# Attention ahead of a routed expert layer on one core: packed inputs, quarter-array scores, softmax sums from a column of ones, and a later weight split

## The chip, the cores and the metric

The kernel runs on one core of a Trainium2 chip. The metric is the device time in microseconds (us) of one execution. A core has five engines that run their own instruction streams side by side: PE (TensorE, matrix products into the accumulator banks called PSUM; PEld is its weight loading), DVE (VectorE), ACT (ScalarE), POOL (GpSimd) and SP (SyncE, which here issues the transfers). Sixteen DMA engines move the data that these streams ask for.

## What is computed

Three parts follow each other. First attention with 4 batches, 8 heads, 576 positions and 64 features a head, in a causal window of 64 positions. Then every one of the 2304 tokens goes to the one of 8 experts that its gate chooses (512 to 1024 to 512 features). Last comes a layer of 512 to 2048 to 512 features with the activation h * cos(h).

```python
def _attn_ref(q, k, v) -> np.ndarray:
    B, H, S, D = q.shape
    window = 64
    scale = 1.0 / np.sqrt(D)
    scores = scale * np.matmul(q, k.transpose(0, 1, 3, 2))
    pos = np.arange(S)
    rel = pos[:, None] - pos[None, :]
    mask = (rel >= 0) & (rel < window)
    scores = np.where(mask, scores, -1000000000.0)
    scores = scores - np.max(scores, axis=-1, keepdims=True)
    attn = np.exp(scores)
    attn = attn / (np.sum(attn, axis=-1, keepdims=True) + 1e-09)
    return np.matmul(attn, v).astype(np.float32)

def reference(**kwargs):
    ...
    x = np.ascontiguousarray(attn_out.transpose(0, 2, 1, 3)).reshape(B * S, H * D)
    x = _moe_ref(x=x, **moe_kwargs)
    return _moe2_ref(x=x, **moe2_kwargs)
```

## The kernel before

The attention works on 18 tiles of 128 tokens. A tile holds two blocks of 64 tokens (`c` is 0 or 1), and a block sees its own 64 keys and the 64 before it. The 8 heads are 4 pairs (`pr`), and `r` says which head of a pair. A loop over `t` runs a software pipeline: the scores of tile `t`, the transposes and the product with the values of tile `t - 1`, the gate's logits of tile `t - 2`, the routing of tile `t - 3`, and the id tables of tile `t - 4`. The order of the instructions on PE, DVE, ACT and SP is that of the program text (`manual_schedule`), so each of these engines works its list in order and waits at the first instruction that isn't ready.

What a tile does, with the lines of the kernel before:

- `load` (L150 to L152) fetches q of the one head of each pair, the keys (each tile its own and the 64 before, so keys between two tiles come twice), and q of the other head. `load_v` (L160) fetches the values in two transfers, one a block. The zeros of `qz` around a head's q let a product over all 128 rows give that head's scores alone. Loads run three tiles ahead, values two.
- `stA` (L173) makes 16 products of 128 rows and 64 columns, 128 wide. Each shows as two instructions, so 32 a tile. `peak` (L191, DVE) adds the mask and takes the maximum, `soft` (L207, ACT) is the exponential, and its accumulator gives the sum of a row in a second instruction (ACTIVATION_READ_ACCUMULATOR).
- `stB` (L223) transposes on PE, `evB` takes the first half out of PSUM on DVE (L230) and the second on ACT (L232), `stC` (L241) multiplies by the values, `norm` (L254 to L259, DVE) divides by the sums.
- `stD` and `stE` (L272 to L283) turn the tile and make the gate's logits; `route`, `gate`, `stF`, `rank` and `stH` find experts and ranks. GpSimd does two small operations a tile (L358, L360).
- Expert 0's weights come as four pieces `wst[c]` of 1 MB at tiles 1, 5, 9 and 13 (L515). Each piece is cut into quarters; of each quarter ACT makes the upper part (L577) and DVE, through `early_lo`, the rest (L115). The 16 quarters are spread over tiles 3 to 17.
- Products of a first slot of expert 0 (`work0`, L477) fill PE's gaps near the end. The last tile's ids go through `ids_part` (L387) and a product to the list `gix`; gathers by that list bring the first slot's tokens, and `mX` (L718) turns them. From there the expert part and the last part are PE work.

PSUM has 8 banks that all stages share in turn.

Of the kernel before, what the change touches and what calls it, by code (L numbers as in the profile page):

```python
# [17 lines left out]
P = 128  # L18
# [13 lines left out]
FILL = ((0, 4, 0, 0), (3, 3, 0, 2), (0, 4, 0, 4), (0, 0, 24, 0), (0, 0, 0, 0))  # L32
NS = NT - 1
# [4 lines left out]
ROW = DM + 1  # L38
NQ = N // P * E // 2
# [9 lines left out]
def kernel(ctx: ExitStack, tc: tile.TileContext, a: dict, out: bass.AP, dbg=None):  # L49
# [33 lines left out]

# [19 lines left out]
    # an expert's weights, as they come and as two parts of 12 bits; expert 0 ahead of the routing  # L103
# [10 lines left out]
    def split_lo(c, w=slice(0, 2048)):  # L114
        nc.vector.tensor_tensor(hl[c][:, 1, w], wst[c][:, w], hl[c][:, 0, w].bitcast(F32), op=ALU.subtract)  # L115

# [6 lines left out]
    # keeps the tensor engine's clock up while it has nothing else to do  # L123
# [8 lines left out]
    # a head's q, with zeros where the other head of its pair has its rows  # L132
    qz = [t4.tile([P, 2, 4, P], F32, name=f"qz{i}", bufs=1) for i in range(4)]
    for i in range(4):
        for r in range(2):
            nc.gpsimd.memset(qz[i][(1 - r) * D : (1 - r) * D + D, r], 0.0)

    def blkinfo(i):
        offs = []
        for c in range(2):  # L140
            b, jb = divmod(2 * i + c, 9)
            offs.append(b * SP + jb * D)
        return offs

    def load(i):
        o0, o1 = blkinfo(i)
        w = o1 - o0 + P
# [7 lines left out]
        st[i] = dict(q=q, k=k, off=(0, o1 - o0))  # L155

    def load_v(i):
        st[i]["v"] = v = t4.tile([P, 2, DM], F32, tag="v", name=f"v{i}", bufs=5)
        for c, o in enumerate(blkinfo(i)):
            nc.sync.dma_start(out=v[:, c, :], in_=a["v"][o : o + P, :])  # L160

    def stA(i):
# [8 lines left out]
        for r in range(2):  # L171
            for pr, c in ((pr, c) for pr in range(4) for c in range(2)):
                nc.tensor.matmul(  # L173
                    sb[r][c * D : c * D + D, pr * P : pr * P + P],
                    s["q"][:, r, pr, c * D : c * D + D],
                    s["k"][:, pr, s["off"][c] : s["off"][c] + P],
                    start=True,
                    stop=True,
                )
# [3 lines left out]
        s["su"] = sm.tile([P, 8], F32, tag="su", name=f"su{i}")  # L183
# [19 lines left out]
    def soft(i, r):  # L203
        s = st[i]
        for pr in range(4):
# [7 lines left out]
                accum_out=s["su"][:, hh : hh + 1],  # L213
# [12 lines left out]
    def evB(i, r):  # L226
        s = st[i]
        dst = s["pT"][:, r * 4 : r * 4 + 4, :].rearrange("p a b -> p (a b)")
        if r == 0:
            nc.vector.tensor_copy(dst, s["pb"][r])  # L230
        else:
            nc.scalar.activation(dst, s["pb"][r], AF.Copy)  # L232

    def stC(i):
        s = st[i]
        ob = psum(f"o{i}")
        for r in range(2):
            for pr in range(4):
                h = 2 * pr + r
# [8 lines left out]
        s["ob"] = ob  # L248

    def norm(i):  # L250
        s = st[i]
        ob = s["ob"]
        ri = sm.tile([P, 8], F32, tag="ri", name=f"ri{i}")
        nc.vector.tensor_scalar(ri, s["su"], 1e-9, None, ALU.add)  # L254
        yield
        nc.vector.reciprocal(ri, ri)
        yield
        xo = t2.tile([P, ROW], F32, tag="xo", name=f"xo{i}", bufs=5)
        nc.vector.tensor_tensor(  # L259
            xo[:, :DM].rearrange("p (a r d) -> p a r d", r=2, d=D),  # L260
            ob[:, :].rearrange("p (a r d) -> p a r d", r=2, d=D),
            ri[:, :].rearrange("p (r a) -> p a r", r=2).unsqueeze(3).to_broadcast([P, 4, 2, D]),
            op=ALU.mult,
        )
        s["xo"] = xo
        yield
# [10 lines left out]
    def stE(i):  # L277
# [6 lines left out]
        s["l"] = lb[:, :E]  # L284

    # steps of VectorE's, a step of another chain between each two of them
# [34 lines left out]
    # ids by expert and rank: a token's row of 128 ranks and its place there as 0 and 1,  # L321
    # summed over the tokens by a product, with the middle of the ids taken off
    idt = {}

    def stF(i):
        s = st[i]
        rb = psum(f"r{i}")
        nc.tensor.matmul(rb[:, :E], onesb, accs, start=True, stop=False)
# [754 lines left out]
```

## Time and profile before

| what | us |
|---|---|
| three runs, without a profile: median | 843.57 |
| lowest, highest | 839.75, 844.72 |
| span of the profiled execution, first to last instruction | 837.9 |

The page gives no time for the profiled execution other than its span; the three runs lie 1.9 to 6.8 us above it. The profile shows one execution: which instruction ran when on which engine, what an engine waited for, and what the DMA engines moved. A duration of one PE instruction includes the pipeline, so the pace is read from the starts. DMA share is the mean busy share of the 16 DMA engines; it can come out somewhat above 1.

### The profile page before, as it was taken

To read this page: it belongs to the slowest core of one execution; us is meant where nothing else is said; L and a number is where in the kernel's file an instruction comes from. 1 tells how busy PE (TensorE), PEld (TensorE's weight loads), DVE (VectorE), ACT (ScalarE), POOL (GpSimd) and SP (SyncE) were. 2 spreads that over 40 slices of the span, in tenths; PEclk is the share of its full clock that TensorE was granted. 3 is DMA by queue.
4 is the path that set the end of the run, shared out by engine and by line. 5 is a ranking of instruction groups with operands and counts; after the bars stand their busy time and mean duration, and the time that the engine had idled before them with its cause. 6 is when DMAs were issued, how large, how long until landed. Compare 5 with 4: busy or idle time off the path is not lost. (4 is left out here: it accounts for less than half of the span.)

```text
span 837.9 us, 15164 instructions
## 1 busy us (share of the span) xinstructions
PE 807.4 (96%) x5233; PEld 700.6 (84%) x5233; DVE 521.0 (62%) x1350; ACT 432.7 (52%) x1045; POOL 108.2 (13%) x119
## 2 busy tenths in 40 slices
PE   7897998999999999999899999999999999999995
PEld 5887876888888888888789999999999999999994
DVE  4786976688457479964378755555555555555552
ACT  5796863454344345453367654454545445445442
POOL 2221322122112122221000010010001001001001
PEclk9998999999999999999999999999999999999998
DMA  9999926889747689871335110100001010001001
GB/s 247 298 302 309 292 82 233 284 302 336 247 144 284 230 270 301 295 277 36 104 106 159 39 38 1 38 30 8 15 24 39 1 38 38 2 1 39 1 0 39
DMA packets 46788, 115.80 MB, mean 138 GB/s; under 512 B 5422, under 2 KB 14638, under 8 KB 42608
## 3 DMA queue, kind: packets, MB, share of 16 engines
q1 hardware_dynamic: 41280, 98.73, 37.0%
q0 software_dynamic: 5280, 16.02, 5.5%
q8 instruction: 43, 0.70, 0.4%
q14 instruction: 41, 0.34, 0.1%
q10 hardware_dynamic: 144, 0.02, 0.0%
HBM read 161.38 MB, written 23.88 MB: 221 GB/s over the span
## 5 line engine op out<-in xcount | busy, mean ns | idle before, releaser
L760 PE MATMUL m<-hl,mhT 128*128 128x512 f32 x528 | 130.5, 403 | 2.7 <-DVEq L899 2.7
L713 PE MATMUL m<-hl,mxT 128*128 128x512 f32 x528 | 129.4, 400 | 0.9 <-DVEq L695 0.7
L940 DVE SCALAR_TENSOR_TENSOR r<-ki,h 128x384 f32<-128x384 int32 x96 | 53.1, 553 | 109.3 <-ACT ki L938 109.3
L760 PEld LDWEIGHTS m<-hl,mhT 128*128 128x128 f32 x528 | 98.8, 191 | 25.6 <-issue 2.9
L713 PEld LDWEIGHTS m<-hl,mxT 128*128 128x128 f32 x528 | 97.8, 188 | 24.0 <-ACTq L695 0.9
L934 PE MATMUL h<-x,wx 128*128 128x384 f32 x576 | 109.5, 339 | 0.0
L934 PE MATMUL h<-x,hl 128*128 128x384 f32 x576 | 109.2, 339 | 0.0
L713 PE MATMUL acc<-wx,g 128*128 128x512 f32 x432 | 108.8, 397 | 0.0
L713 PE MATMUL acc<-hl,g 128*128 128x512 f32 x432 | 108.3, 394 | 0.2 <-DVE g L955 0.2
L934 PEld LDWEIGHTS h<-x,wx 128*128 128x128 f32 x576 | 102.8, 188 | 4.0
L934 PEld LDWEIGHTS h<-x,hl 128*128 128x128 f32 x576 | 102.8, 188 | 3.8
L938 ACT ACTIVATE ki<-h 128x384 int32<-128x384 f32 x96 | 47.0, 490 | 110.6 <-PE h L934 110.6
L949 DVE SCALAR_TENSOR_TENSOR r<-q,h 128x384 f32<-128x384 f32 x96 | 53.2, 554 | 65.8 <-ACT q L948 65.8
L713 PEld LDWEIGHTS acc<-hl,g 128*128 128x128 f32 x432 | 80.1, 188 | 15.6 <-DVE g L955 0.7
L947 ACT ACTIVATE q<-r 128x384 f32<-128x384 f32 x96 | 50.4, 526 | 81.3 <-DVE r L941 81.3
L713 PEld LDWEIGHTS acc<-wx,g 128*128 128x128 f32 x432 | 79.5, 188 | 15.4 <-DVE g L955 0.3
L115 DVE TENSOR_TENSOR hl<-wst,hl 128x2048 fp32r<-128x2048 f32 (+1 forms) x44 | 74.5, 1705 | 10.8 <-ACT hl L698 7.0
L73 POOL DMA_INDIRECT out_dram<-o,tid x18 | 17.9, 996 | 350.3 <-ACT o L972 346.7
L207 ACT ACTIVATE p<-sm,nm 128x128 f32<-128x128 f32 x144 | 55.6, 390 | 5.3 <-DVE nm L191 5.3
L941 DVE SCALAR_TENSOR_TENSOR r<-ki,r 128x384 f32<-128x384 int32 x96 | 53.8, 560 | 3.3
L955 DVE TENSOR_TENSOR g<-r,g 128x384 fp32r<-128x384 f32 x96 | 52.9, 551 | 0.6 <-ACT g L954 0.6
L948 ACT ACTIVATE q<-q 128x384 f32<-128x384 f32 x96 | 50.4, 525 | 3.0
(171 smaller groups left out, 1001.9 us busy)
## 6 DMA issues: line engine op xcount, KB each, us to landing
wst<-in_we_dram SPq DMA_DIRECT2D x98, 1024.0 KB
w<-in_wf_dram SPq DMA_DIRECT2D x32, 512.0 KB
v<-in_v_dram SPq DMA_DIRECT2D x36, 256.0 KB
wf<-wr SPq DMA_DIRECT2D x32, 256.0 KB
raw<-wf SPq DMA_DIRECT2D x32, 256.0 KB
k<-in_k_dram SPq DMA_DIRECT2D x16, 384.0 KB
xs<-xo SPq DMA_DIRECT2D x18, 256.5 KB
yl<-yc SPq DMA_DIRECT2D x6, 769.5 KB
```

The source lines that it names most:

```text
L115: nc.vector.tensor_tensor(hl[c][:, 1, w], wst[c][:, w], hl[c][:, 0, w].bitcast(F32), op=ALU.subtract)
L207: nc.scalar.activation(s["p"][:, hh, :], s["sq"][:, hh, :], AF.Exp, bias=s["nm"][:, hh : hh + 1], scale=-1.0, accum_out=s["su"][:, hh : hh ...
L713: nc.tensor.matmul(acc, x[:, i, xk], w[:, j, wk], start=(first and n == 0), stop=(last and n == 2))
L760: nc.tensor.matmul(pb, ms[s]["hT"][c][:, i, k], w, start=(m == 0), stop=(m == 23))
L934: nc.tensor.matmul(hb, w[:, wi, o : o + P], xb[i]["x"][k][:, xi, :], start=(k == 0 and n == 0), stop=(k == 3 and n == 2))
L938: nc.scalar.activation(ki, hb, AF.Copy, scale=0.15915494309189535)
L940: nc.vector.scalar_tensor_tensor(r, ki, -PI_A, hb, ALU.mult, ALU.add)
L941: nc.vector.scalar_tensor_tensor(r, ki, -PI_B, r, ALU.mult, ALU.add)
L947: nc.scalar.activation(q, r, AF.Sin, scale=0.5)
L948: nc.scalar.activation(q, q, AF.Square, scale=1.4142135623730951)
L949: nc.vector.scalar_tensor_tensor(r, q, 1.0, hb, ALU.subtract, ALU.mult, reverse0=True)
L955: nc.vector.tensor_tensor(g[:, 1, :], r, g[:, 0, :].bitcast(F32), op=ALU.subtract)
```

## The change

Each tile's q and keys lie side by side in one array and come in one transfer of 512 KB; its values come in one transfer of 520 KB, with a column of ones after each head's 64 features. A tile's keys come once: the 64 keys before a tile are read from the tile before (`kp`). The products of the scores use 64 rows and 64 columns each, four quarters of the array, 24 products instead of 16, those of block 0 cut into two of 64 wide. The zeros around q are gone. `soft` has no accumulator; the sums come out of `stC` as the column of ones, in two PSUM banks instead of one, and `norm` reads them there (two additions, one reciprocal, two multiplications). Both halves of `evB` are on ACT. The rank's result shares a bank with the logits. The weight pieces are fetched at tiles 3, 7, 14 and 16. Their first 8 quarters are split one a tile at tiles 6 to 13, the rest on GpSimd instead of DVE; the last 8 come after the last tile's scores, at t = 18, 19 and 20 (3, 3 and 2), on ACT and DVE. The filler products at t = 0 are of another type and number. The first slot's gather goes to `wst[1]` instead of `wst[2]`. The rest of the diff removes comments.

```diff
+WLOAD = (3, 7, 14, 16)
+SPLITS = {6 + n: (n,) for n in range(8)} | {NT: (8, 9, 10), NT + 1: (11, 12, 13), NT + 2: (14, 15)}
...
-        q = qz[i % 4]
-        k = t4.tile([P, 4, 256], F32, tag="k", name=f"k{i}", bufs=4)
-        nc.sync.dma_start(out=q[:D, 0], in_=a["q"][i, 0])
-        nc.sync.dma_start(out=k[:, :, :w], in_=a["k"][:, :, o0 : o0 + w])
-        nc.sync.dma_start(out=q[D:, 1], in_=a["q"][i, 1])
+        qk = t4.tile([P, 2, 4, P], F32, tag="qk", name=f"qk{i}", bufs=5)
+        nc.sync.dma_start(out=qk[:, :, :, :].rearrange("p a b c -> p (a b c)"), in_=a["qkv"][i, :, : WQ + WK])
...
-        for c, o in enumerate(blkinfo(i)):
-            nc.sync.dma_start(out=v[:, c, :], in_=a["v"][o : o + P, :])
+        nc.sync.dma_start(out=v[:, :, :, :].rearrange("p a b c -> p (a b c)"), in_=a["qkv"][i, :, WQ + WK :])
...
-        for r in range(2):
-            for pr, c in ((pr, c) for pr in range(4) for c in range(2)):
-                nc.tensor.matmul(
-                    sb[r][c * D : c * D + D, pr * P : pr * P + P],
-                    s["q"][:, r, pr, c * D : c * D + D],
-                    s["k"][:, pr, s["off"][c] : s["off"][c] + P],
+        for pr in range(4):
+            for c, at, k in ((0, 0, s["kp"][:, pr, D:]), (1, 0, s["k"][:, pr, :]), (0, D, s["k"][:, pr, :D])):
+                for r in range(2):
+                    h = slice(r * D, r * D + D)
+                    nc.tensor.matmul(
+                        sb[r][c * D : c * D + D, pr * P + at : pr * P + at + k.shape[1]],
+                        s["q"][h, pr, c * D : c * D + D],
+                        k[h],
...
-                accum_out=s["su"][:, hh : hh + 1],
...
-        if r == 0:
-            nc.vector.tensor_copy(dst, s["pb"][r])
-        else:
-            nc.scalar.activation(dst, s["pb"][r], AF.Copy)
+        nc.scalar.activation(dst, s["pb"][r], AF.Copy)
...
-                        ob[c * D : c * D + D, h * D : h * D + D],
+                        ob[c * D : c * D + D, pr * DV : pr * DV + DV],
                         s["pT"][:, r * 4 + pr, c * D : c * D + D],
-                        s["v"][:, c, h * D : h * D + D],
+                        s["v"][:, c, 2 * pr + r, :],
...
+        for r in range(2):
+            nc.vector.tensor_scalar(ri[:, r], s["ob"][r][:, :, D], 1e-9, None, ALU.add)
+            yield
...
+                load_v(1)
                 load(2)
-                load_v(1)
...
-                idle(4, "idle3")
+                idle_r([224] * 7 + [256] * 6 + [512] * 3, "idle3")
...
-            for n in range(max(0, t - 3) * 16 // 14, min(16, max(0, t - 2) * 16 // 14)):
+            for n in SPLITS.get(t, ()):
                 c, w = n // 4, slice(n % 4 * 512, n % 4 * 512 + 512)
                 nc.scalar.activation(hl[c][:, 0, w], wst[c][:, w], AF.Copy)
-                early.append((c, w))
+                if t < NT:
+                    split_lo(c, w, nc.gpsimd)
+                else:
+                    early.append((c, w))
```

## Rows read from the trace of the kernel before

**Rows 1.** Stretches: busy us of each engine (instructions), granted PE clock, DMA share, GB/s.
```profile
16.04:107.93 91.89, 82.64 (x1469) 75.95 (x1466) 73.45 (x521) 73.79 (x317) 20.95 (x29) 0.96 1.02 291
72.40:79.10 6.70, 5.07 (x63) 4.96 (x65) 2.91 (x21) 5.38 (x22) 1.42 (x2) 0.50 1.09 281
107.93:130.39 22.46, 18.89 (x208) 14.75 (x206) 17.04 (x108) 10.90 (x36) 7.44 (x10) 1.00 0.35 109
130.39:837.90 707.51, 693.87 (x3424) 601.80 (x3424) 424.86 (x683) 340.16 (x661) 75.41 (x69) 0.99 0.35 117
200.00:400.00 200.00, 200.00 (x962) 163.39 (x961) 134.54 (x164) 88.02 (x150) 41.86 (x33) 1.00 0.69 236
```

**Rows 2.** Timeline of DVE: first mask operation of tile 2 and of tile 17.
```profile
16.04 0.29 DVE L191 CUSTOM_DVE_ANT_0 sm<-s,cst 128x128 f32<-128x128 f32 x1 [0.83 <-PE s L173]
...
107.93 0.28 DVE L191 CUSTOM_DVE_ANT_0 sm<-s,cst 128x128 f32<-128x128 f32 x1
```

**Rows 3.** Transfers up to 110 us: SP's queue (packets, MB, share of 16 engines), then issues, KB each.
```profile
q1 hardware_dynamic: 20448, 30.02, 96.4%
...
v<-in_v_dram SPq DMA_DIRECT2D x36, 256.0 KB
k<-in_k_dram SPq DMA_DIRECT2D x16, 384.0 KB
qz<-in_q_dram SPq DMA_DIRECT2D x36, 128.0 KB
wst<-in_we_dram SPq DMA_DIRECT2D x4, 1024.0 KB
xs<-xo SPq DMA_DIRECT2D x14, 256.5 KB
```

**Rows 4.** Waits from 16.04 to 107.93: who for whom, us in total, times, longest.
```profile
ACT hl L577 <- DMA wst<-in_we_dram: 8.6, 3, 5.3
...
PE o L241 <- ACT pT L232: 5.0, 3, 3.4
```

**Rows 5.** Timeline of PE, one tile: start, us, what.
```profile
60.14 1.97 PE L173 MATMUL s<-k,qz 128*64 128x128 f32 x32
62.04 1.09 PE L223 MATMUL pt<-cst,p 128*128 128x128 f32 x8
...
63.56 1.15 PE L241 MATMUL o<-v,pT 128*64 128x64 f32 x32
64.54 0.59 PE L283 MATMUL l<-wg,xT 128*64 128x8 f32 x16
...
65.30 0.88 PE L173 MATMUL s<-k,qz 128*64 128x128 f32 x12
```

**Rows 6.** Timeline of ACT in one tile: two evictions, then exponentials.
```profile
57.91 0.60 ACT L274 ACTIVATE xT<-xT 128x512 f32<-128x512 f32 x1
58.41 0.39 ACT L207 ACTIVATE p<-sm,nm 128x128 f32<-128x128 f32 x1
58.70 0.19 ACT L207 ACTIVATION_READ_ACCUMULATOR p<-sm,nm 128x1 f32 x1
58.79 0.39 ACT L207 ACTIVATE p<-sm,nm 128x128 f32<-128x128 f32 x1
```

**Rows 7.** Groups by line, 16.04 to 107.93: count, busy us, mean ns, idle before.
```profile
L241 PE MATMUL o<-v,pT 128*64 128x64 f32 x480 | 18.2, 228 | 7.6 <-ACT pT L232 5.0 <-DVE pT L230 2.1 <-ACT xT L274 0.5
...
L360 POOL TENSOR_SCALAR op<-cst,qf 128x128 f16<-128x128 f32 x14 | 11.2, 798 | 0.0
...
L115 DVE TENSOR_TENSOR hl<-wst,hl 128x512 fp32r<-128x512 f32 x14 | 9.6, 682 | 3.2 <-ACT hl L577 3.2
```

**Rows 8.** Timeline behind the last tile: DVE, and PE's first turned slot.
```profile
120.86 0.17 DVE L291 MAX8 mx<-l 128x8 f32<-128x8 f32 x1 [0.27 <-PE l L283]
...
124.67 0.42 DVE L387 CAST ids<-idt 72x256 f16<-72x256 f32 x1 [0.51 <-PE idt L375]
...
130.39 0.65 PE L718 MATMUL mx<-cst,xg 128*128 128x128 f32 x4 [1.47 <-DMA xg<-xs,gix]
```

More of the change, by code (lines that the diff above doesn't have):

```diff
@@ L112, in hilo, with split_lo @@
             nc.vector.tensor_tensor(tl, pb, th.bitcast(F32), op=ALU.subtract)
-    def split_lo(c, w=slice(0, 2048)):
-        nc.vector.tensor_tensor(hl[c][:, 1, w], wst[c][:, w], hl[c][:, 0, w].bitcast(F32), op=ALU.subtract)
+    def split_lo(c, w=slice(0, 2048), eng=None):
+        (eng or nc.vector).tensor_tensor(hl[c][:, 1, w], wst[c][:, w], hl[c][:, 0, w].bitcast(F32), op=ALU.subtract)
     actx = ExitStack()
@@ L130, in idle, with idle_r @@
             nc.tensor.matmul(b, nul, bc(nul, [P, 4, P], 1), start=True, stop=True)
[L133 to L152 removed]
+    nulr = t4.tile([P, 512], F32R, name="nulr", bufs=1)
+    nc.vector.memset(nulr[:, :].bitcast(F32), 0.0)
+    def idle_r(widths, name):
+        b = psum(name)
+        for w in widths:
+            nc.tensor.matmul(b[:, :w], nulr[:, :P], nulr[:, :w], start=True, stop=True)
+    def load(i):
+        qk = t4.tile([P, 2, 4, P], F32, tag="qk", name=f"qk{i}", bufs=5)
+        nc.sync.dma_start(out=qk[:, :, :, :].rearrange("p a b c -> p (a b c)"), in_=a["qkv"][i, :, : WQ + WK])
         if i == 0:
             nc.sync.dma_start(out=cst[:, : 4 * P], in_=a["cst"][:, : 4 * P])
[L155 removed]
+        st[i] = dict(q=qk[:, 0], k=qk[:, 1], kp=st[i - 1]["k"] if i else qk[:, 1])
     def load_v(i):
[L158 to L160 removed]
+        st[i]["v"] = v = t4.tile([P, 2, H, DV], F32, tag="v", name=f"v{i}", bufs=4)
+        nc.sync.dma_start(out=v[:, :, :, :].rearrange("p a b c -> p (a b c)"), in_=a["qkv"][i, :, WQ + WK :])
     def stA(i):
@@ L170, in stA @@
         sb = [psum(f"s{i}_{r}") for r in range(2)]
-        for r in range(2):
-            for pr, c in ((pr, c) for pr in range(4) for c in range(2)):
-                nc.tensor.matmul(
-                    sb[r][c * D : c * D + D, pr * P : pr * P + P],
-                    s["q"][:, r, pr, c * D : c * D + D],
-                    s["k"][:, pr, s["off"][c] : s["off"][c] + P],
-                    start=True,
-                    stop=True,
-                )
+        for pr in range(4):
[6 more added lines that the diff above has]
+                        k[h],
+                        start=True,
+                        stop=True,
+                    )
         s.update(sb=sb, mk=mk)
         s["nm"] = sm.tile([P, 8], F32, tag="nm", name=f"nm{i}")
-        s["su"] = sm.tile([P, 8], F32, tag="su", name=f"su{i}")
         s["p"] = t4.tile([P, 8, P], F32, tag="p", name=f"p{i}")
@@ L247, in stC @@
                     )
-        s["ob"] = ob
+            s["ob"].append(ob[:, : 4 * DV].rearrange("p (a d) -> p a d", d=DV))
     def norm(i):
         s = st[i]
-        ob = s["ob"]
-        ri = sm.tile([P, 8], F32, tag="ri", name=f"ri{i}")
-        nc.vector.tensor_scalar(ri, s["su"], 1e-9, None, ALU.add)
-        yield
[L256 to L266, printed above, removed]
+        ri = sm.tile([P, 2, 4], F32, tag="ri", name=f"ri{i}")
+        xo = t2.tile([P, ROW], F32, tag="xo", name=f"xo{i}", bufs=5)
+        s["xo"] = xo
+        for r in range(2):
+            nc.vector.tensor_scalar(ri[:, r], s["ob"][r][:, :, D], 1e-9, None, ALU.add)
+            yield
+        nc.vector.reciprocal(ri[:, :, :].rearrange("p a b -> p (a b)"), ri[:, :, :].rearrange("p a b -> p (a b)"))
+        yield
+        for r in range(2):
+            nc.vector.tensor_tensor(
+                xo[:, :DM].rearrange("p (a r d) -> p a r d", r=2, d=D)[:, :, r, :],
+                s["ob"][r][:, :, :D],
+                ri[:, r].unsqueeze(2).to_broadcast([P, 4, D]),
+                op=ALU.mult,
+            )
+            yield
     def stD(i):
@@ L326, in stF @@
         s = st[i]
-        rb = psum(f"r{i}")
-        nc.tensor.matmul(rb[:, :E], onesb, accs, start=True, stop=False)
-        nc.tensor.matmul(rb[:, :E], trib, s["ohb"], start=False, stop=True)
-        s["rb"] = rb
+        nc.tensor.matmul(s["rb"], onesb, accs, start=True, stop=False)
+        nc.tensor.matmul(s["rb"], trib, s["ohb"], start=False, stop=True)
         if i == T0:
@@ L341, in rank @@
         pm = sm.tile([P, E], F32, tag="pm", name=f"pm{i}")
-        nc.vector.tensor_tensor(pm, s["rb"][:, :E], ohb, op=ALU.mult)
+        nc.vector.tensor_tensor(pm, s["rb"], ohb, op=ALU.mult)
         yield
@@ L423, in counts @@
         yield
-    xg0 = wst[2][:, :ROW]
+    xg0 = wst[1][:, :ROW]
     xT0 = t4.tile([P, 2, 4, P], F32R, tag="xt0", name="xt0", bufs=1)
@@ L512 @@
                 load_v(t + 2)
-            if t < 16 and t % 4 == 1:
-                c = t // 4
+            if t in WLOAD:
+                c = WLOAD.index(t)
                 nc.sync.dma_start(out=wst[c], in_=a["we"][c])
```

27 lines of the change are left out of this document (16 added, 11 removed).

## The prediction

> **What bounds the kernel now.** I read the stretches first. From the last turn of the routing on, 130.39 to 837.90 us, PE is busy for 693.87 of 707.51 us at nearly full clock [rows 1]. The change touches no instruction there, so I carry these 707.5 us over unchanged; the change can only move the moment at which they begin. Ahead of it lie the 18 tiles. Tile 2's first mask operation starts at 16.04 and tile 17's at 107.93 [rows 2], 91.89 us for 15 tiles, 6.13 a tile. Behind tile 17 comes a tail of 22.46 us.
>
> Three things pace the tiles. First the DMA engines: their share is 1.02 in this stretch [rows 1]. SP's queue moved 30.02 MB in 110 us at 96.4% of all 16 engines [rows 3], so 30.02 / (0.964 x 110 us) = 283 GB/s is what full engines gave with these transfers. By tile 17's scores these had to be in: q and keys 11,776 KB, 17 tiles' values 8,704, weights 4,096, 14 rows of `xs` 3,591 going out, and the constants, left out here and below: 28,167 KB or 28.8 MB, 102 us at that rate. The tiles came no faster than their data. Second, what shows it: ACT waited 8.6 us for weight pieces, 5.3 at once [rows 4], because a piece queues behind loads. ACT works in order, so the eviction behind it was late and PE waited 3.4 us. After that idle time the granted clock was 0.50 from 72.4 to 79.1, the level of 1.2 GHz; PE's 5.07 busy us there [rows 1] cost about 2.5 too many. Third, PE itself: in a tile without a long wait its starts run from 60.14 to 65.30, 5.16 us with no gap worth the name [rows 5]. DVE and ACT have 73.45 and 73.79 busy us in 15 tiles, 4.9 each [rows 1]. So four resources lie between 4.9 and 6.1, and a gain on one goes only as far as the next.
>
> **The transfers.** A tile's q and keys go from 640 KB to 512, its values from 512 to 520; 1,152 to 1,032 KB. By tile 17's scores I count 9,216 + 8,840 KB of inputs, two weight pieces (those of tiles 14 and 16 queue behind tile 17's load), 12 rows of `xs`: 23,182 KB, 23.7 MB. At 283 GB/s that is 84 us; the stretch 200 to 400, with larger rows, ran 236 GB/s at a share of 0.69 [rows 1], 342 at full engines, which gives 69. Both with some 3 us ahead of the first byte and behind the last: 72 to 87. Rows grow from 768 bytes and 2 KB to 4 KB, so I take the middle, 80, and the transfers stop pacing the tiles if compute puts tile 17 later than that.
>
> **PE's scores.** Before, 32 instructions of 128 columns take 62.04 - 60.14 = 1.90 us, 59 ns each with two column halves side by side [rows 5]. Now there are 24 products, 48 instructions, on four quarters. No row shows quarters. Below: four at once halve the stream, 0.95. Above: the row halves do not overlap, 1.90, with a little for the cut product 1.96. Nearest is the product with the values, 32 instructions of 64 columns in 64.54 - 63.56 = 0.98 us, 30.6 ns each [rows 5]; 48 of these are 1.47, and I take that. The rest of PE's tile stays at 65.30 - 62.04 = 3.26 (65 columns for 64, one bank more). So 4.73, between 4.21 and 5.22.
>
> Here a page speaks against cutting. The Trainium skill, TensorEngine Tiling (Array Packing), section Instruction Overhead, says that each product carries about 60 cycles whatever its width and that one should not take a tiling factor from a small dimension. By it an estimate for 48 instructions is 48 x 25 ns = 1.2 us, 0.27 a tile or 4 us in all less than my value; the row's 30.6 ns is a little more than the page's 25.
>
> **ACT.** An exponential starts every 58.79 - 58.41 = 0.38 us; its accumulator read starts 0.29 behind it [rows 6]. Without the read the next can start there: 0.29 each if so, 0.38 if not. An eviction takes 58.41 - 57.91 = 0.50 to the next start. With three evictions, 8 exponentials and the gate's, put at the same price, a tile is 4.1 us, 4.6 with a weight quarter (0.5), which 8 tiles have; 0.8 more at the upper end, 4.9 and 5.4. I take the lower, since the read starts where the engine was free. **DVE** loses an eviction and a weight part, both of the 0.68 kind [rows 7], and gains a second addition and multiplication, about 0.3: 4.9 - 1.36 + 0.3 = 3.8, hidden behind PE. One wait is new: the first addition of `norm` now waits for `stC`, where the sum was ready long before. Behind it on DVE stand the rank and the next tile's masks, for which ACT waits; DVE's 1.1 of spare time a tile covers it. Without that cover it would cost what `stC` takes, 1 us a tile, and ACT's exponentials would be late next.
>
> **GpSimd** takes 8 weight parts, one a tile. Bounds: 0.68 as on DVE, or 512/128 x 0.80 = 3.2 by its own operation [rows 7]. With the 20.95 / 15 = 1.4 it has now [rows 1] that is 2.1 to 4.6 of a tile of 4.9: nothing on the path. I take 3.2; behind it on its queue are only the next tile's two operations, for which `stH` waits a tile later.
>
> **Pace.** PE's ordinary waits, 7.6 less the 3.4, are 0.28 a tile [rows 4, 7]. Those on DVE's eviction go with it, so I add 0.17: 4.9 a tile, bounds 4.55 (ACT's mean of 4.4, with the same 0.17) and 5.5 (PE's or ACT's upper end). 15 x (6.13 - 4.9) = **18.4 us less**. The 8.6 us of weight waits and the low clock are in this sum, since the pieces now have three tiles or more, of a queue that isn't full.
>
> **Start.** Tile 2 waited for its keys [rows 2]. Up to them the queue now has 2,576 KB in place of 2,432 (values of tile 1 moved ahead): 0.5 us more at 283 GB/s, 1.1 less at 342, and the scores are 0.4 shorter. I take **1.0 less** (0 to 1.5), nearer the larger rows' rate: tile 2 at 15.0, tile 17 at 15.0 + 73.5 = 88.5, behind the transfers' 80. The fillers at t = 0 stand between scores 0 and 1, where PE waits anyway; if they are longer they delay tile 1, inside the same bound.
>
> **Tail.** Tile 17's two weight quarters leave, about 1.2 us with the shorter scores. But at t = 19, 20 and 21 DVE gets 3, 3 and 2 parts of 0.68 [rows 7] in its own order: 2.0 ahead of tile 17's routing, where DVE now waits 0.27; 2.0 among the steps that make the last ids; 1.4 ahead of the id copy, where it waits 0.51 [rows 8]. Behind those stand the gathers and PE's first turn at 130.39, which waits for the gather [rows 8]. 5.4 - 0.8 of idle time is 4.6; less 1.2 is 3.4. Bounds 0 (all hidden) and 4.7. ACT's quarters there fall in its idle time (10.90 busy of 22.46 [rows 1]). I take **3.5 more**.
>
> **Sum.** -18.4 - 1.0 + 3.5 = -15.9. On the span 837.9 that is 822.0; on the median of the runs, 843.57, it is **827.7**. The profiled execution is known by its span alone, so I take the difference as the same for both.
>
> **Rivals.**
> - The quarters don't run side by side, or ACT keeps 0.38 an exponential: a pace of 5.5. For it: no row shows quarters, and nothing excludes either. Against: column halves overlap now. Tile 17 at 97.5, turn at 123.5, 6.9 us less than before: 836.7.
> - The packing doesn't do what it is for: transfers still pace, at the rate tiles got before, 1,636 KB in 6.13 us or 273 GB/s. A tile then needs 1,516 KB, 5.7 us: 15.0 + 85.3 + 26.0 = 126.3, 4.1 less: 839.5. For it: the share of 1.02. Against: the weight pieces come later, and rows of 4 KB.
> - All low ends: 14.5 + 15 x 4.55 + 22.5 = 105.2, 25.2 less: 818.4. For it: ACT and PE would then be balanced, as DVE, ACT and PE nearly are now; against: the tail's DVE work has little idle time to hide in.
> - Slower: GpSimd's weight part becomes the bound of tiles 6 to 13, since `stH` needs GpSimd's two operations. It must cost 8.4 us more than before, 24.3 more than my sum, 3.0 a tile: 7.9 a tile, so 6.5 us for one part, twice the upper bound above. Then 852. Speaking for it: no two-input operation of GpSimd is in the trace.
>
> On that last rival the Trainium skill, GPSIMD Engine Reference, section 4.1, says that elementwise work belongs on the vector engine and is about twice as slow on GpSimd. An estimate by it is 1.4 us a part; no run here shows it, and it speaks against the move without making it the bound.
>
> **Chances.** My sum 0.58, the slow quarters or exponentials 0.13, transfers 0.08, all low ends 0.10, GpSimd 0.05, the tail eating the rest (no change) 0.06. About 1% is what a measurement of this kernel can tell from no change: below 835.1 is faster. That is my sum, the low ends and half of the first two rivals, which lie near that edge: 0.78. The other half and the eaten gain are the same, 0.17; slower 0.05. My sum's own range, with scores of 1.2 to 1.7 us and the tail's bounds, is 821 to 833; taking in the first rival and the low ends, 817 to 838.
>
> **What would show it.** Right: first masks about 4.9 us apart, no ACT wait for `wst`, a DMA share clearly under 1 in the tiles, scores of about 1.5 us, clock 1.00 throughout, the turn some 26 us behind tile 17. Wrong: the share still at 1 (transfers), scores at 1.9 (quarters), starts of exponentials still 0.38 apart, `stH` waiting for GpSimd, or a stretch behind the turn that isn't 707 us.

## The result and the profile after

The changed kernel takes 831.75 us (median of 4 runs, 831.65 to 834.95) where the kernel before took 841.66 beside it: a ratio of 0.989, with a 95% interval of 0.986 to 0.992. The profiled execution has a span of 829.9 us, 8.0 less than before. The direction and the range held; the size did not, since 15.9 us less were forecast and 9.9 came.

The stretches of the changed kernel, with the columns of [rows 1] (length, then busy us of PE, PEld, DVE, ACT and POOL with instructions, granted clock, DMA share, GB/s):

```profile
14.54:96.39 81.85, 70.48 (x1694) 64.34 (x1693) 65.15 (x523) 66.04 (x202) 30.97 (x37) 0.98 0.86 286
96.39:121.89 25.50, 21.55 (x204) 16.11 (x203) 19.59 (x116) 14.74 (x37) 8.42 (x11) 0.88 0.36 108
121.89:829.90 708.01, 694.31 (x3425) 602.04 (x3423) 424.74 (x683) 339.84 (x661) 76.73 (x68) 0.99 0.35 116
```

They begin with the first mask operations of tile 2 and tile 17, the same rows as in [rows 2] (timeline of DVE):

```profile
14.54 0.28 DVE L190 CUSTOM_DVE_ANT_0 sm<-s,cst 128x128 f32<-128x128 f32 x1
...
96.39 0.28 DVE L190 CUSTOM_DVE_ANT_0 sm<-s,cst 128x128 f32<-128x128 f32 x1
```

Three of the four stretches came out as forecast: tile 2 at 14.54 (15.0), tail 25.50 (26.0), last part 708.01 (707.5). The fourth did not: (96.39 - 14.54) / 15 = 5.46 us a tile, where 4.9 was forecast. The missing 15 x 0.56 = 8.4 us are all there. The transfers are not what holds it: up to 110 us SP's queue moved 28.12 MB at 74.1% of the engines, or 345 GB/s at full engines, against 96.4% and 283 GB/s in [rows 3]; in the tiles alone their share is 0.86 for 1.02:

```profile
q1 hardware_dynamic: 8374, 28.12, 74.1%
...
q8 instruction: 16, 0.26, 0.9%
...
v<-in_qkv_dram SPq DMA_DIRECT2D x18, 520.0 KB
qk<-in_qkv_dram SPq DMA_DIRECT2D x18, 512.0 KB
```

Nor do any weight waits of ACT remain [rows 4]. What PE waits for instead, from 16 to 97 us (who for whom, us in total, times, longest):

```profile
PE l L325 <- DVE ohb L299: 4.6, 8, 0.9
PE s L173 <- issue: 3.6, 2, 3.2
PE o L236 <- issue: 1.3, 2, 1.1
PE l L279 <- issue: 0.9, 1, 0.9
PE l L324 <- DVE ls L296: 0.5, 2, 0.2
```

So there are two new things in the tiles. In some tiles the rank product waits for the one-hot row `ohb`. And five times PE stops for no other engine at all ("issue"), 5.8 us together. In the tail the clock of 0.88 is a stretch of 0.50 from 115.69 us to the turn, which the account of the tail below takes up; the prediction's sign of a clock of 1.00 throughout did not hold.

**The stop near 54 us.** Timeline of PE around the longest stop:

```profile
53.88 0.27 PE L173 MATMUL s<-qk 64*64 64x128 f32 x1
57.33 0.43 PE L173 MATMUL s<-qk 64*64 64x128 f32 x6 [3.18 <-issue]
```

PE stands in the middle of a tile's score products, whose operands are all there. Afterwards the granted clock is 0.50, the level of 1.2 GHz, from 57.67 to 61.08, and tiles 9 and 10, counted from first mask to next first mask, take 8.13 and 6.33 us. Queue 8 carries instructions, 16 KB a packet. The transfers from 48.6 to 54.8 us, then those from 54.8 to 57.3 (queue: packets, MB, share):

```profile
q1 hardware_dynamic: 604, 1.84, 83.9%
...
q1 hardware_dynamic: 165, 0.44, 98.4%
q14 instruction: 1, 0.01, 3.2%
q8 instruction: 1, 0.02, 2.3%
```

No packet came in the first stretch. One started at 54.85, when PE already stood, and PE went on 2.48 us later. Now count instructions from one such stop to the next (stretches that begin and end at a stop, columns as above):

```profile
21.45:26.75 5.30, 4.95 (x126) 4.54 (x126) 4.22 (x36) 3.62 (x13) 1.45 (x2) 1.00 1.00 337
26.75:48.95 22.20, 19.89 (x504) 18.15 (x504) 18.70 (x151) 19.51 (x63) 8.75 (x11) 1.00 0.90 304
48.95:57.32 8.37, 5.05 (x126) 4.46 (x126) 4.17 (x36) 4.73 (x15) 4.75 (x6) 1.00 0.90 261
57.32:88.83 31.51, 27.45 (x628) 25.37 (x628) 26.34 (x213) 26.20 (x80) 13.32 (x15) 0.95 0.77 246
```

126 products and 126 weight loads, and with 4 semaphore instructions that this view does not count, 256. Then, counted in the same way, 4, 1 and 5 times 256. From the start of the trace the stops come behind 705, 961, 1985, 2241 and 3521 instructions of PE, always 705 plus a multiple of 256. The Trainium skill, Runtime: NRT & Kernel Launch, section Instruction fetch mechanics, says that an engine's instructions come in blocks of 256 through a DMA queue of its own and that crossing a block's end is mostly hidden; the trace agrees with the 256 and not with the hiding, which failed by up to 3.18 us here. The kernel before has one such stop, at the same count (341 + 341 and 23 instructions of PE's sequencer, not counted in this view, are 705), in its stretch up to it and its timeline:

```profile
0.00:28.28 28.28, 23.45 (x341) 18.45 (x341) 14.66 (x106) 16.63 (x72) 5.38 (x15) 1.00 0.97 265
```

```profile
28.32 0.33 PE L223 MATMUL pt<-cst,p 128*128 128x128 f32 x1 [0.67 <-issue]
```

It ran about 200 PE instructions a tile of 6.13 us, so a block of 256 lasted 7.8 us; the changed kernel runs 230 in 5.46, 6.1 us a block. A packet starts on average 3.2 us after PE passes the end of a block (3.0 in the kernel before; 5.9 at most now, 5.2 before), and what it brings, needed at the next end, serves PE some 2.2 to 2.6 us after the start. The delay hardly changed; the time that hid it did.

**The wait for `ohb`.** GpSimd's weight part, then DVE's `ohb`, in tile 11:

```profile
65.00 1.27 POOL L119 TENSOR_TENSOR hl<-wst,hl 128x512 fp32r<-128x512 f32 x1
```

```profile
65.40 0.91 DVE L299 TENSOR_SCALAR ohb<-cst,ixf 128x8 bf16<-128x8 f32 x1
```

An operation of 8 columns takes 0.91 us and ends with GpSimd's part, at 66.3. In tiles without a part beside it, it takes 0.22 to 0.23; in six of the eight tiles with a part it takes 0.53 to 0.91. Other operations of DVE that begin while a part runs keep their time: the masks, whose scores are in PSUM, 0.28 us, `ls`, a TENSOR_SCALAR of the same shape from PSUM, 0.22, and the cast `ixf`, one column from SBUF, 0.15.

### The profile page after: what moved, and what is told of

It is laid out like the page before. It is cut to its first block, busy times and chain, and to the rows that moved or that the text cites. A ratio compares the mean times of both kernels' runs of the same rounds, so it can differ in the third digit from the quotient of the medians.

```text
span 829.9 us, 15578 instructions
## 1 busy us (share of the span) xinstructions
PE 799.6 (96%) x5533; PEld 691.8 (83%) x5533; DVE 515.3 (62%) x1361; ACT 427.8 (52%) x919; POOL 116.4 (14%) x119
## 4 chain that ended last, share of the span: by engine, by line
PE 49%; issue 1%; ACT 1%; DVE 0%; POOLq 0%; POOL 0%; DVEq 0%; ACTq 0%
PE acc L712 24%; PE h L933 24%; PE yt L814 1%; PE m L759 0%; ACT hl L833 0%; POOLq L1080 0%; POOL out_dram L77 0%; DVE r L939 0%; ACT o L971 0%; DVE r L940 0%; DVE g L954 0%; DVE r L948 0%; ACT q L947 0%; ACT q L946 0%; ACT ki L937 0%
## 5 line engine op out<-in xcount | busy, mean ns | idle before, releaser
L119 DVE TENSOR_TENSOR hl<-wst,hl 128x2048 fp32r<-128x2048 f32 (+1 forms) x36 | 69.0, 1933 | 8.1 <-ACT hl L697 7.7
L683 POOL DMA_INDIRECT xg<-xs,gix x24 | 30.2, 1258 | 156.7 <-ACT my L766 148.7
```

Source lines behind the costliest of these rows:

```text
L119: (eng or nc.vector).tensor_tensor(hl[c][:, 1, w], wst[c][:, w], hl[c][:, 0, w].bitcast(F32), op=ALU.subtract)
L683: nc.gpsimd.indirect_dma_start(out=xg[s % NG][:, :], out_offset=None, in_=xs[:, :], in_offset=bass.IndirectOffsetOnAxis(ap=gix[:, s : s + ...
```

## The experiments

Every run is compared with the kernel before on its own chip; as not all ran on the same chip, runs are best compared with each other by their ratios. "Stops" are PE's waits above 0.15 us without a releaser up to tile 17's first mask, "delay" is the mean start of instruction packets behind the block's end in front; both are counted from one profile each. "PE" is the number of PE's products, weight loads and semaphore instructions in a tile. Of e6 and e9, which leave out loads, only the columns of the tiles count.

| run | us | ratio, 95% interval | us a tile | PE a tile | stops us | delay us | tail us |
|---|---|---|---|---|---|---|---|
| kernel before | 841.66 | 1 | 6.13 | 200 | 0.7 | 3.0 | 22.5 |
| changed kernel | 831.75 | 0.989 (0.986 to 0.992) | 5.46 | 230 | 5.8 | 3.2 | 25.5 |
| e1 `ohb` from PSUM | 830.59 | 0.988 (0.985 to 0.990) | 5.48 | 230 | 6.7 | 3.0 | 25.6 |
| e2 gate last | 833.98 | 0.992 (0.990 to 0.995) | 5.46 | 230 | 8.1 | 3.3 | 25.2 |
| e3 pieces spread | 830.12 | 0.990 (0.986 to 0.993) | 5.43 | 230 | 7.1 | 3.3 | 25.8 |
| e4 stream shifted | 832.01 | 0.989 (0.986 to 0.992) | 5.49 | 230 | 6.2 | 2.8 | 25.0 |
| e5 16 products | 830.14 | 0.985 (0.983 to 0.988) | 5.52 | 204 | 5.4 | 3.3 | 25.0 |
| e6 fewer loads | 815.32 | one run | 5.06 | 229 | 0.6 | 1.6 | 24.6 |
| e7 weights early | 829.59 | 0.983 (0.978 to 0.988) | 5.72 | 230 | 9.1 | 3.3 | 23.1 |
| e8 quarters alone | 840.27 | 0.999 (0.997 to 1.001) | 6.09 | 198 | 0.5 | 3.0 | 22.6 |
| e9 = e6 + e1 | 814.14 | one run | 4.92 | 229 | 0.7 | 2.0 | 25.1 |
| e10 all | 826.79 | 0.983 (0.980 to 0.986) | 5.20 | 188 | 1.0 | 3.3 | 23.6 |
| e11 all, gate in 8 | 831.02 | 0.986 (0.983 to 0.988) | 5.75 | 205 | 10.2 | 3.6 | 23.5 |
| e12 all, gate last | 833.41 | 0.989 (0.985 to 0.993) | 5.50 | 204 | 8.5 | 3.3 | 23.6 |

### e1: the one-hot row from PSUM

```diff
-        nc.vector.tensor_scalar(ohb, iota_e, ixf, None, ALU.is_equal)
+        nc.vector.tensor_scalar(ohb, l, mx[:, 0:1], None, ALU.is_equal)
```

> The changed kernel with one operand pair swapped: the one-hot row of a token's expert (`ohb`) is made by comparing the logits in PSUM with their maximum, in place of comparing `iota_e` in SBUF with the index; where two logits are equal it would mark both. Its size, its place in VectorE's order and GpSimd's weight parts stay. Theory A (this SBUF-to-SBUF operation, and it alone, stands still while GpSimd's weight part runs): `ohb` takes about 0.2 us in every tile, the 0.58 to 0.86 us waits of TensorE's rank product for `ohb` in tiles 7, 8 and 11 to 14 go, those tiles come 0.5 us faster, 3 to 4.5 us in all. Rival A1 (any VectorE operation is slowed beside GpSimd, or the delay has another cause): `ohb` stays at 0.9 and the time does not move. Rival A2 (the wait was only in the place of another): `ohb` gets short, but the tiles stay at 5.1 to 5.2 us, under 1 us in all. The 3.2 us stop of TensorE near 54 us should be there again by any of them.

The line's durations (minimum/median/maximum ns) in the changed kernel, then in e1:

```profile
L299 DVE TENSOR_SCALAR ohb<-cst,ixf x18: 224/229/907, 19.4 to 110.4; 128x8 bf16<-128x8 f32 x18
```

```profile
L299 DVE TENSOR_SCALAR ohb<-l,mx x18: 215/220/223, 19.3 to 110.7; 128x8 bf16<-128x8 f32 x18
```

The place in DVE's order and GpSimd's parts were the same; with the operand in PSUM no `ohb` is lengthened. That is theory A for the mechanism: it isn't VectorE as a whole that stands beside GpSimd, but an operation of this kind with its operand in SBUF. The Trainium skill, SBUF — State Buffer, section Who interferes with whom, says that `tensor_scalar` from SBUF can take a port pair that VectorE shares with GpSimd, which whoever came first holds for its whole instruction; the 0.91 us beside the 1.27 and the 0.22 from PSUM agree. The time is another matter: tiles 7, 11 and 14 came to 4.6 to 5.0 us, the stops rose from 5.8 to 6.7, the pace stayed and 831.75 against 830.59 cannot be told apart. The time went as rival A2 has it.

### e2: the gate's steps last

```diff
                 on(1) and norm(t - 1),
-                on(3) and not last and gated(t - 3),
             )
+            weave(on(3) and not last and gated(t - 3))
```

> The changed kernel with the two steps of `gated` (1/sum of the gate and the row's store) behind the end of `norm` and `rank` in VectorE's order instead of between them. Theory C (VectorE stands 0.4 to 1.0 us a tile waiting for the gate's exponential with `norm` queued behind it, so the next masks start late): the wait of the line with the gate's sum in front of `norm` goes; tiles without a weight part (5.0 to 5.3 us) come to 4.6 to 4.8, 2 to 4 us in all. Rival C1: these waits are in VectorE's spare time, TensorE's own 4.55 us and its waits for `ohb` set the pace, and the time moves by less than 1 us. GpSimd's delay of `ohb` stays by either.

DVE's wait in the changed kernel, from 14 to 96.4 us, is gone in e2:

```profile
DVE gs L312 <- ACT ex L307: 7.9, 11, 1.0
```

Tile 5 came from 5.03 to 4.55 us, as theory C has it; tile 6 was at 4.55 before. But DVE's wait for PE's values `o` grew from 2.2 to 6.4 us, the stops rose to 8.1 us in seven places, the pace is the same 5.46 and the time is no better. The time went as C1 has it: what some tiles gained, the stops (2.2 us more) took.

### e3: the weights' pieces spread, and e4: the instructions shifted

e3:

```diff
-WLOAD = (3, 7, 14, 16)
+WLOAD = {3 + n: (n,) for n in range(8)} | {11 + n: (8 + n,) for n in range(3)} | {14: (11, 12), 15: (13, 14), 16: (15,)}
...
-                nc.sync.dma_start(out=wst[c], in_=a["we"][c])
+                nc.sync.dma_start(out=wst[c][:, w], in_=a["we"][c][:, w])
```

> The changed kernel with expert 0's weights loaded in 16 quarters of 256 KB, one a tile from tile 3 on (two a tile at tiles 14 and 15), in place of four pieces of 1 MB at tiles 3, 7, 14 and 16. The splits and all bytes stay. Theory B (TensorE's instruction packets are served late while a 1 MB piece makes the queue of loads long; the packet that ended the stop near 54 us came only when the queue had run empty): no wait of TensorE without a releaser over 0.5 us in tiles 3 to 16, no half clock at 57 us, tiles 9 and 10 at about 5.2 in place of 8.1 and 6.3, 4 to 5 us in all. Rival B1 (the packet is late by its place in TensorE's instructions): a stop of 3 us stays near tile 9 or 10, under 1 us of change. Rival B2 (a queue that is full in every tile): ScalarE waits for quarters, or several smaller stops, same or slower by up to 4 us.

e4:

```diff
-                idle(10, "idle0")
+                b0 = psum("idle0")
+                for _ in range(40):
+                    nc.tensor.matmul(b0[:, :P], nul, nul, start=True, stop=True)
...
-                idle_r([224] * 7 + [256] * 6 + [512] * 3, "idle3")
+                idle_r([112] * 14 + [128] * 12 + [256] * 6, "idle3")
```

> The changed kernel with the same filler columns at t = 0 in more, narrower products: 40 of 128 columns for 10 of 512, and 32 for 16, so that all of TensorE's later instructions stand 92 places (about 0.4 of a packet of instructions) further back. Theory B (the stop belongs to the backlog of loads behind tile 7's weight piece): a stop stays between 50 and 57 us, of 2 to 4 us. Rival B1 (the stop belongs to a place in the instructions): it comes about 2 us earlier in the stream, in another operation, at its full 3.2 us, and elsewhere nothing changes. Rival B3 (it is the chance of the moment): it is gone or stands in quite another tile. The time moves by less than 2 us by B and B1, by -5 by B3.

Both tell the same. In e3 the long stop and the half clock at 57 us are gone, but eight stops of 0.25 to 1.63 us make 7.1, and packets are no earlier on average (3.3): theory B, that a single piece of 1 MB makes the packet late, is wrong as an account of the time; B2 of that run comes nearest. In e4 92 instructions more stood in front, and the stops came again behind 705, 961, 1217, 1729, 1985 and 3521 instructions, so 92 earlier in the program; the one at 1985 was 0.74 us, the longest 2.16 at 87.94. None of e4's three accounts holds as it stood. Where PE can stop is given by the count of instructions. How long it stops is not.

### e5: 16 score products

```diff
...
+            if i % 5:
+                o, w = (i % 5 - 1) * (WQ + WK) + WQ + pr * P + D, WQ + WK - D
+                two = ring[:, o : o + 2 * w].rearrange("p (a b) -> p a b", b=w)[:, :, :D]
+                parts = ((0, 0, two), (1, 0, s["k"][:, pr, :]))
...
```

> The changed kernel with the five `qk` buffers side by side in one tile, so that a tile's 128 keys of its first column half, half of them in the buffer before, are one operand with a stride: 16 score products in place of 24 in all tiles but 0, 5, 10 and 15, 64 rows of TensorE for 96, a tile 200 for 232. Same bytes, same columns. Theory B2, as the first four runs left it (TensorE stops only at every 256th instruction, until some 2.4 us behind the start of the next packet of instructions; that packet starts 1 to 7 us behind the boundary before): a block then lasts 1.28 tiles, the stops of 5.8 to 8.1 us in all fall under 2.5, tiles 2 to 17 take 4.9 to 5.1 us each for 5.46, 4 to 7 us less in all. Rival: the stops were only in the place of other waits (the loop through VectorE, the gate and the exponentials at 5.0, GpSimd's part), and the time falls by less than 2 us. Scores: 0.72 us if each instruction costs what it costs now (1.08 / 48), about 1.0 if the columns do.

Timeline of PE: scores as 24 products in tile 15, then as 16 in tile 16 (start, us, what):

```profile
85.15 1.15 PE L182 MATMUL s<-ring 64*64 64x64 f32 x48
86.23 1.09 PE L230 MATMUL pt<-cst,p 128*128 128x128 f32 x8
...
89.70 1.10 PE L182 MATMUL s<-ring 64*64 64x128 f32 x32
90.74 1.09 PE L230 MATMUL pt<-cst,p 128*128 128x128 f32 x8
```

86.23 - 85.15 = 1.08 and 90.74 - 89.70 = 1.04 us, up to the next kind of product: with a third fewer instructions the scores take the same time, so their columns cost, not their number. There were three stops where there had been five, but 5.4 us in all, two of them 2.49 and 2.63 with packets 5.5 and 6.1 us behind, and from the end of each the clock was 0.50 for 3.4 us. The forecast of B2 (stops under 2.5 us, 4.9 to 5.1 a tile) missed: the pace is 5.52. The ratio is 0.985 for the changed kernel's 0.989, and the intervals overlap.

### e6: fewer loads, and e9: the same with the one-hot row from PSUM

```diff
...
     def load_v(i):
+        if i >= 4:
+            st[i]["v"] = vs[i % 4]
+            return
...
```

> The changed kernel with the values of tiles 4 to 17 not loaded (tile i takes those of tile i modulo 4): 7,280 KB less for the DMA engines, the rest as it was. Attention and so the routing of those tiles are other than the reference's, so only the stretch up to the turn counts. Theory B2 (a packet of instructions waits for the loads): packets start under 1.5 us behind the boundary before them, TensorE's stops without a releaser are under 1 us in all, the clock stays at 1.00, tile 17's first mask is at 88 to 91 us. Rival (the packet's delay is TensorE's own, or that of its place): stops of 5 us or more at the same places, rows 705 + 256 n.

> e6 (values of tiles 4 to 17 not loaded, so attention and routing are not the reference's there) with the one-hot row of e1, compared from the logits in PSUM. In e6 TensorE had 0.6 us of stops without a releaser and tiles 7 to 14 took 5.04 to 5.33 us with waits of 0.57 to 0.86 for `ohb`. If GpSimd's part is a second cause of its own, hidden in e1 only because TensorE then stood at a block of instructions: tiles 7 to 14 come to 4.6 to 4.8 us, tile 17's first mask 3 to 4.5 us earlier than in e6 (90.33), so 86 to 87.5. If the wait is only in the place of another (rival): the tiles stay at 5.0 or more, under 1.5 us in all.

e6 in its stretch of tiles, and PE's waits there:

```profile
14.44:90.33 75.89, 67.93 (x1698) 62.57 (x1698) 66.27 (x522) 66.11 (x203) 30.94 (x37) 1.00 0.70 210
```

```profile
PE l L331 <- DVE ohb L305: 6.6, 12, 0.9
PE l L285 <- issue: 0.6, 1, 0.6
```

The same instructions, a third less to transfer, a DMA share of 0.70 for 0.86: packets start 1.6 us behind for 3.2, one stop of 0.6 is left, the clock is 1.00 throughout and the pace is 5.06. So the transfers delay the packets. And e9:

```profile
14.46:88.25 73.79, 68.51 (x1696) 62.56 (x1696) 61.34 (x522) 65.79 (x202) 30.90 (x37) 1.00 0.70 216
```

2.1 us less than e6, DVE 4.9 us less busy: `ohb` is a cause of its own, worth less than the 3 to 4.5 us expected, because tiles 7 to 10 and 12 still took 4.99 to 5.14, with DVE waiting up to 1.0 us for the gate's exponential (10.5 us in all), as in the changed kernel. `ohb` itself takes 0.22 in every tile of e9, yet PE still waits 4.1 us for it, 6.6 in e6, since DVE comes to it late. (88.25 - 14.46) / 15 = 4.92 us a tile, tile 17 at 88.25. The prediction had said 4.9 and 88.5; how much of that agreement is luck is said below, under the pace.

### e7: the weights' schedule of before, and e8: the quarters alone

e7, on the changed kernel:

```diff
-WLOAD = (3, 7, 14, 16)
-SPLITS = {6 + n: (n,) for n in range(8)} | {NT: (8, 9, 10), NT + 1: (11, 12, 13), NT + 2: (14, 15)}
+WLOAD = (1, 5, 9, 13)
+SPLITS = {t: range((t - 3) * 16 // 14, min(16, (t - 2) * 16 // 14)) for t in range(3, NT + 4)}
...
-                if t < NT:
-                    split_lo(c, w, nc.gpsimd)
-                else:
-                    early.append((c, w))
+                early.append((c, w))
```

> The changed kernel with the weights' schedule of the kernel before: pieces at tiles 1, 5, 9 and 13, 16 quarters split over tiles 3 to 17, the low parts on VectorE; packed inputs, quarter scores and the sums' column stay. If the later schedule is what won the stretch of tiles (weight waits of 8.6 us and the low clock before): tile 17's first mask is 4 us or more later than 96.4, the tail 3 us shorter, 0 to 4 us slower than the changed kernel. If the schedule is worth nothing once the inputs are packed (rival): no wait of ScalarE for `wst`, no `ohb` of 0.9 us, the tail 3 us shorter than 25.5, and the time 2 to 5 us below the changed kernel's.

e8, on the kernel before:

```diff
-                    s["q"][:, r, pr, c * D : c * D + D],
-                    s["k"][:, pr, s["off"][c] : s["off"][c] + P],
+                    s["q"][h, r, pr, c * D : c * D + D],
+                    s["k"][h, pr, s["off"][c] : s["off"][c] + P],
```

> The kernel before with its 32 score instructions on 64 rows each (the half of `qz` that is not zero) in the order that puts four quarters side by side; nothing else. If the transfers pace the tiles of the kernel before (the prediction's reading): the scores fall from 1.90 to about 1.0 us, the starts of tiles hardly move, TensorE waits more for keys and weight pieces, 0 to 3 us less in all. Rival (TensorE's own time paced them): 0.9 us a tile, 12 us or more less.

With the early schedule e7 is not slower than the changed kernel. ACT waits for a weight piece once, from 15 to 101 us,

```profile
ACT hl L573 <- DMA wst<-in_we_dram: 1.5, 1, 1.5
```

against 8.6 us in [rows 4]; the stops are 9.1 us (tiles 5 to 9 have one each), and the tail is 2.4 us shorter, 23.1. So with the early schedule kept, the rest of the change takes most of the weight waits away; that it is the packing in it is likely and not shown, since no run has the packed inputs alone. Its four runs lie from 824.2 to 834.1, so what moving the weights is worth in time can't be said.

In e8 the scores fell to 1.03 us (55.69 to 56.72 in its timeline of PE) from 1.90 [rows 5], and the stretch got no shorter:

```profile
16.54:107.89 91.35, 76.03 (x1456) 66.52 (x1457) 73.13 (x520) 73.25 (x315) 21.04 (x29) 0.91 1.02 291
```

91.35 us for 91.89 [rows 1], at the same DMA share of 1.02. The granted clock was 0.50 for 17.1 us, where it was for 6.8 in the kernel before; as an estimate from these two, the 10.2 us more at half clock take back 5 us at most, and 15 x 0.87 = 13 us were to be had. So in the kernel before it was the transfers that set the pace.

### e10 to e12: put together

```diff
...
+WLOAD = {3 + n: (n,) for n in range(14)} | {NT - 1: (14, 15)}
+SPLITS = {6 + n: (n,) for n in range(12)} | {NT: (12, 13), NT + 1: (14, 15)}
...
-            for c in range(2):
-                h = slice(c * D, c * D + D)
-                nc.tensor.matmul(lb[h, :E], s["xT"][:, kk, h], wg[:, kk, :], start=(kk == 0), stop=(kk == 3))
+            nc.tensor.matmul(lb[:, :E], s["xT"][:, kk], wg[:, kk, :], start=(kk == 0), stop=(kk == 3))
```

(with the edits of e1 and e5 and the transfers by quarters of e3; 12 quarters in place of 8 are now split beside the tiles. e11 takes the gate's lines back, e12 is e11 with the edit of e2)

> What the runs point to, together: 16 score products (e5), weights loaded in quarters, one a tile from tile 3 on (e3), the one-hot row from PSUM (e1), the gate's logits in 4 products of 128 columns instead of 8 of 64 (8 instructions and 8 weight loads fewer a tile), and 12 quarters in place of 8 split beside the tiles, which leaves 4 of VectorE's parts in the tail. A tile is then 184 rows of TensorE in place of 232 and a block of 256 lasts 1.4 tiles. If the instruction supply and `ohb` were what kept the pace at 5.46: stops under 2 us in all, 4.6 to 4.9 us a tile, 8 to 12 us off the stretch of tiles and 1 to 2 off the tail, 819 to 824 us. Rival: the loop through VectorE, the gate's exponential and `norm` keeps 5.0 a tile: 825 to 827.

> e10 with the gate's logits in 8 products of 64 columns again, as in the changed kernel: in e10 the 4 wide ones took 0.92 us a tile for 0.52. A tile is 200 rows of TensorE. If TensorE's own 4.9 us set e10's ordinary tiles of 5.04: 4.6 to 4.7 a tile unless VectorE's wait for the gate's exponential (0.95 us in e10) keeps them at 5.0; stops without a releaser a little more than e10's 0.98, under 3. Same to 5 us below e10.

> e11 with the steps of `gated` behind `norm` and `rank` (the edit of e2). Theory C (the loop through the gate's exponential holds VectorE and so the next masks at 5.0 us a tile once TensorE gets its instructions; e2 could not show it, since TensorE stood 8.1 us for instructions): tiles at 4.5 to 4.7, 3 to 6 us below e11. Rival C1 (the wait is VectorE's spare time, and faster tiles only come to the next block of instructions): within 1.5 us of e11, with stops without a releaser of 3 us or more.

e10 has the lowest median of the complete kernels, 826.79 us, 1.7% below the kernel before; e7 has the same ratio, with runs that scatter more. Its stretch of tiles and PE's waits:

```profile
14.46:92.48 78.02, 74.39 (x1382) 67.04 (x1381) 61.80 (x521) 67.44 (x205) 33.63 (x40) 1.00 0.91 294
```

```profile
PE l L331 <- DVE ohb L306: 1.5, 5, 0.5
PE o L245 <- issue: 1.0, 2, 0.5
```

Its wide gate products cost PE more, 0.92 us a tile (48.70 - 47.78) for 0.52, and ordinary tiles are a steady 5.04, more than the 4.6 to 4.9 expected, and the time is that of the run's rival, 825 to 827. Yet only 1.0 us of stops is left, and the clock is 1.00. e11 gives PE the 0.4 us back and 16 instructions a tile more. Its ordinary tiles are 4.6 to 5.0, and it has lost it all at two ends of blocks, 3.57 and 4.80 us, each with a clock of 0.50 behind it. In e12 five tiles take 4.55 to 4.59, more than in any other run, so the tiles are as theory C has them; but PE stands 4.39, 1.50 and 2.65 us, and the time is not below e11's:

```profile
PE s L182 <- issue: 4.4, 1, 4.4
PE l L288 <- issue: 4.2, 2, 2.7
```

Expected was that PE's own time matters more than these 16 instructions; it was the other way. One profile each shows this, and the interval of e10 overlaps with those of e11 and, barely, e12, so e10's lead over them is likely and not settled.

## Why the prediction was right and wrong

- **Transfers.** Right. The share fell from 1.02 to 0.86 and none of the tiles waits for its data; full engines gave 345 GB/s, near the upper of its two rates. e8 shows the other half, that the transfers had set the pace.
- **Scores.** The cut into quarters works, 1.90 to 1.08 us; 1.47 was taken. The row it was taken from, 30.6 ns an instruction of the values' product [rows 5], was the wrong one to go by: e5 shows that the number of instructions does not set this time. The forecast's lower bound, 0.95 with four quarters side by side, was the near one. The Trainium skill, TensorEngine Tiling (Array Packing), section Instruction Overhead, was taken for a price on every product, 1.2 us; its own words, that one column costs what 60 do, make it a floor, and with that e5 agrees: products of 64 columns lie above it, 48 instructions in 1.08 us are 22.5 ns each and not 25, and the cut costs 0.04 us.
- **ACT and DVE.** Four exponentials take 1.27 us, 0.29 to 0.30 each from start to start, as forecast [rows 6]. In the timeline of ACT:

```profile
47.29 1.27 ACT L206 ACTIVATE p<-sm,nm 128x128 f32<-128x128 f32 x4
```

  DVE is busy 65.15 / 15 = 4.34 a tile, not 3.8; 61.34 / 15 = 4.09 where no `ohb` stands (e9).
- **GpSimd.** The part takes 1.27 us, inside its bounds of 0.68 to 3.2 and close to the 1.4 that the prediction estimated by the Trainium skill, GPSIMD Engine Reference, section 4.1. "Nothing on the path" was the first step that failed. The prediction asked who waits for GpSimd's results, not which engine its running holds up. It cost some 0.5 us in the tiles that it met and 2.1 in all, once nothing else held PE (e6 to e9).
- **Pace, the term that was mis-sized:** 18.4 us less was forecast, 91.89 - 81.85 = 10.0 came. The prediction compared four resources, DMA, PE, ACT and DVE, between 4.9 and 6.1 us a tile, and warned that a gain goes only as far as the next. The next was a fifth that it did not list: PE's instructions, 256 at a time, over the DMA engines that also carry the tiles. Taking away loads takes 5.46 to 5.06 (e6), taking away the `ohb` delay too gives 4.92 (e9), which is the forecast. That it agrees so closely is in part luck: PE's scores had been put 0.39 us too long, while PE's waits for `ohb` in e9, 4.1 us in all, come with a wait of DVE for the gate's exponential that the prediction did not have (in e12, without that wait, they are 0.5 us for 3.1 in e11). The profile of before held the sign: one stop of 0.67 us without a releaser, passed over.
- **Start, tail, last part.** Right within 0.5 us each. In the tail DVE's parts delay the ids as forecast: PE waits 1.49 us for them where it waited 0.48. But the turn does not wait for the gather as in [rows 8]. PE's last products ahead of it, in the kernel before and then in the changed kernel, with the turn:

```profile
125.21 0.71 PE L760 MATMUL m_-1_2702<-hl,mhT 128*128 128x512 f32 x2
126.32 2.60 PE L760 MATMUL m_-1_2702<-hl,mhT 128*128 128x512 f32 x10 [0.40 <-DVE mhT L112]
```

```profile
116.34 5.75 PE L759 MATMUL m_-1_2812<-hl,mhT 128*128 128x512 f32 x12
121.89 0.91 PE L717 MATMUL mx<-cst,xg 128*128 128x128 f32 x4
```

  At a granted clock of 0.50 the same 12 products take 5.75 us for 3.31, and the turn follows them without a wait. Where it waits for the gather, it comes 3.5 to 3.9 us behind the first gather's start (kernel before, e10, e12); here it comes 4.9 behind (117.00 to 121.89). As an estimate from these, the low clock cost 1.0 to 1.4 us, and that the tail came out in the middle of its wide bounds is in part luck.
- **Rivals.** The pace of the rival with slow quarters, 5.5, is what came, without slow quarters. GpSimd did not become the bound: PE's `stH` waited for nothing in the tiles.
- **Open.** What makes a packet start 1 us behind the end of a block or nearly 8. Fewer bytes make it earlier on average (e6); smaller pieces do not (e3). The longest single delays, 7.8 and 7.5 us, came in e11 and e12. No run varied the packets themselves.

## What to carry to other kernels

When a change makes an engine's stretch shorter, count its instructions per stretch as well as its time: a gain of 11% in time with 15% more instructions can end at the instruction supply, and the sign is an "issue" wait with a fixed number of instructions, or a multiple of it, between two of them. Fewer, wider instructions may then be worth more than faster ones, as e10 beside e11 suggests without settling it. Work moved to an idle engine needs two questions: who waits for its result, and which operations of other engines stand still while it runs.

## What the runs showed that was not expected

- PE's stops stand only at ends of blocks of 256 of its instructions, in all runs, behind 705 + 256 n, and end 2.2 to 2.6 us (2.8 in the kernel before, 2.7 in e8) after a 16 KB packet starts; the packet itself takes 0.9 to 1.6 us, up to 2.1 in the kernel before.
- With a DMA share of 0.83 to 1.02 in the tiles such a packet starts 2.8 to 3.6 us behind a block's end on average, at 0.70 it is 1.6 to 2.0.
- At the end of 11 of the 12 longest stops (2.16 to 4.80 us) the granted clock was 0.50 for 3.4 or 6.8 us, so a stop cost more than its length; it was 1.00 behind one of 2.17 us in e7 and behind those of 1.63 in e3 and 1.78 in e2, but 0.50 behind 1.33 in e1 and 1.62 in e7.
- A TENSOR_SCALAR of 8 columns from SBUF took 0.70 to 0.91 us in all eight tiles of e6 with a weight part on GpSimd beside it, and 0.22 in all of e1 and e9, where its operand is in PSUM.
- 24 score products of 64 and 128 columns on four quarters take 1.08 us, 16 of 128 take 1.04.
